# Column-halved first weights and keys, DMA-transposed first keys of the second layer, and a new instruction order

## The chip, the cores and the metric

The kernel runs on one core of one Trainium2 chip. The metric is the device time of one execution in microseconds (us); less is better. A core has five instruction queues that run side by side: PE (TensorE, matmuls; its weight loads are shown as PEld), DVE (VectorE), ACT (ScalarE), POOL (GpSimd) and SP (SyncE, which only issues DMAs). Each queue runs its own list strictly in order, and an instruction whose semaphore is not yet up holds everything behind it on its queue.

## The reference

Input `A_x` is 2048 tokens of 512 features in bf16. Four sublayers follow, each a layer norm, a mixing step and a residual: A, B, A, B. Both passes of A and both of B use the same weights.

```python
# A: 32 heads of 16; the tokens are 4 segments of 512
q, k, v = heads(x @ wq), heads(x @ wk), heads(x @ wv)
for s in range(4):
    p = softmax(qs @ ks.T * 0.25 + causal mask)        # inside the segment
    a_mem = (phi(qs) @ M) / (phi(qs) @ z + 1e-6)       # phi(t) = t+1 or exp(t)
    o = g * a_mem + (1 - g) * (p @ vs)
    M, z = M + phi(ks).T @ vs, z + sum(phi(ks))
x = x + concat(o) @ wo
# B: linear attention over all tokens with feature maps
phi_q, phi_k = [softmax(q w), softmax(-q w)], [softmax(k w), softmax(-k w)]
x = x + ((phi_q @ (phi_k.T @ v)) / (phi_q @ sum(phi_k) + 1e-6)) @ wo
```

## The kernel before, in words

**Tiles.** Tokens lie in 16 tiles of 128, four per segment. `X` holds all of them in SBUF. For a segment, `ln` normalises the four tiles (statistics, `xn`) and turns them feature-major, by PE transposes and a copy out of PSUM where `by_pe` says so, otherwise by a DMA transpose from the SP queue. `a_proj` makes keys, queries and values of a segment; `a_att` does scores, exponentials and the products with the values; `a_out` the output projection and the residual. `b_keys`, `b_queries` and `b_out` do the same for B; B's output needs the sums over all tokens, so `b_out` of a layer can start only when `b_keys` has seen the last segment. "Layer" below means one A and one B.

**Keys.** Scores run on 32-row strips of the array, so the keys of even and odd heads are kept apart, zeros in between: `K[:, par, g, token]`, par 0 or 1, g one of four feature groups of 128. There are two ways to fill it. The direct way (`by_pe=(0, 1)`, the first two tiles of the first segment of both layers): PE computes keys feature-major (`kfm`, 16 matmuls of 128 columns a tile) and three scaled copies out of PSUM (`kfm.copy`, L905 and L906) mask them into K; because the values phi(k) need token-major keys too, PE computes the keys a second time (`k`), with `phi_sum` behind it. The other way, all other tiles: PE computes keys token-major (`k`), a copy spreads them into `ktok` (`k.copy`, L563), and a DMA transpose issued by SP writes K (`kT`). A copy `kp` of the diagonal part goes to `KP` in both. In the direct way queries are computed a tile at a time (`q`, 16 matmuls of 128 columns), in the other a pair of tiles and half of the groups at a time (8 matmuls of 256 columns, twice).

**Scores.** A unit of `stages` is 1024 columns of scores for two pairs of PSUM banks; ACT takes two exponentials of 128 x 1024 for it (L1102, 288 in all). In a first segment unit 0 holds the scores of query tile 1 against the odd keys of tile 0 for all four groups; units 1 to 4 hold the diagonals of one group each and the rest.

**Order.** No scheduler runs on the chip. `ORDER` lists all operations by number, in the order in which they join their queues; `ENGINE` gives a letter for each operation that may run on one of several engines (copies out of PSUM on ACT or DVE, masks on DVE or POOL, stores on ACT or SP); `SLOTS` gives buffers. Negative numbers in `ORDER` are dummy matmuls on a tile `warm` of zeros (L1430, `-408` is 25 of them); they wait for the memset of `warm` (operation 20, DVE, L686), and they stand first in the PE queue, ahead of the first transposes. Operations 81 and 82 are the two DVE memsets that clear `ktok` (L751).

**Start.** `setup` loads the first four tiles of x, then the weights of A from the ACT and SP queues: `wk` as two halves of its rows, then `wq` and `wv` in the same way.

Of the kernel before, what the change touches and what calls it, by code (L numbers as in the profile page):

```python
# [14 lines left out]
D = 512  # L15
# [18 lines left out]
    0, 21, 24, 25, 20, 35, 26, 34, 27, 22, 28, 29, 33, 1, 81, 23, 10, 82, 12, 4, 5, 2, 3, 6, 7, 37, 53, 13, 54, 55, 60, 61, 62, 11, 56, 63, 57, 9,  # L34
    -408, 58, 74, 64, 30, 40, 31, 32, 8, -72, 65, 36, 38, 59, 75, 413, 84, 85, 66, 76, 45, 77, 103, 18, 104, 86, 87, 67, 115, 116, 83, 96, 97, 68,
    69, 41, 414, 78, 42, 105, 117, 46, 88, 17, 106, 39, 70, 47, 98, 159, 79, 160, 71, 48, 107, 72, 80, 89, 49, 161, 73, 323, 50, 134, 91, 133, 110,
    121, 90, 325, 324, 92, 135, 93, 136, 326, 327, 328, 177, 142, 178, 179, 94, 140, 139, 143, 102, 95, 137, 145, 144, 146, 147, 162, 122, 182, 141,
    108, 123, 180, 329, 109, 330, 51, 19, 124, 163, 167, 207, 165, 111, 118, 183, 212, 208, 164, 166, 332, 99, 334, 52, 333, 112, 100, 125, 119, 168,
    184, 101, 127, 44, 120, 181, -40, 192, 197, 335, 193, 130, 185, 186, 131, 171, 172, 187, 113, 336, 128, 169, 138, 114, 170, 416, 126, 417, 331,
    1112, 188, 132, 214, 189, 229, 173, 194, 148, 209, 337, 174, 129, 230, 231, 199, 14, 210, 362, 198, 195, 213, 190, 363, 191, 364, 149, 232, 726,  # L40
    150, 196, 211, 175, 15, 201, 200, 368, 216, 1105, 176, 215, 202, 43, 338, 369, 339, 203, 366, 424, 341, 204, 353, 233, 237, 365, 217, 218, 219,
    253, 220, 151, 205, 370, 258, 152, 153, 374, 375, 221, 206, 154, 234, 254, 372, 371, 238, 727, 415, 376, 244, 245, 426, 246, 367, 373, 427, 342,
    343, 428, 418, 344, 235, 354, 429, 355, 340, 236, 347, 222, 241, 242, 419, 356, 359, 155, 243, 420, 239, 156, 226, 247, 248, 240, 421, 262, 260,
    264, 259, 16, 724, 227, 735, 377, 249, 733, 228, 250, 265, 256, 425, 263, 266, 725, 251, 255, 252, 728, 729, 436, 257, 223, 224, 225, 261, 437,
    434, 345, 389, 435, 438, 439, 267, 360, 386, 274, 268, 346, 279, 269, 348, 270, 731, 349, 440, 441, 271, 357, 442, 286, 361, 275, 276, 287, 387,
    277, 288, 430, 378, 281, 388, 431, 379, 380, -70, 283, 383, 422, 390, 391, 272, 285, 734, 1113, 278, 273, 736, 423, 730, 392, 350, 737, 295, 284,
    351, 395, 280, 358, 732, 289, 290, 396, 452, 453, 157, 296, 397, 384, 282, 1114, 158, 398, 300, 399, 307, 455, 297, 454, 298, 308, 385, 291, 738,
    739, 404, 405, 456, 292, 400, 463, 309, 304, 401, 305, 1103, 402, 406, 464, 410, 352, 411, 293, 457, 299, 310, 458, 302, 311, 306, 301, 303, 574,
    742, 412, 740, 312, 466, 465, 381, 313, 408, 382, 579, 432, 460, 461, 467, 294, 393, 314, 315, 1104, 575, 1106, 433, 407, 548, 403, 459, 549,
    559, 564, 552, 580, 743, 462, 316, 553, 577, 581, 409, 394, 560, 582, 744, 741, 468, 550, 556, 562, 558, 745, 557, 537, 551, 538, -35, 604, 576,  # L50
    469, 578, 320, 539, 321, 748, 566, 317, 318, 322, 605, 609, 631, 561, 749, 319, 583, 445, 584, 585, 563, 586, 565, 587, 471, 472, 610, 443, 588,
    567, 446, 636, 444, 447, 632, 750, 589, 594, 568, 569, 448, 570, 571, 751, 752, 799, 1107, 590, 606, 591, 643, 753, 644, 645, 607, 800, 763, 608,
    611, 612, 754, 595, 450, 449, 473, 801, 546, 572, 592, 764, 593, 613, 614, 547, 615, 616, 765, 628, 802, 638, 573, 617, 542, 778, 544, 618, 543,
    540, 451, 555, 629, 596, 787, 598, 767, 788, 597, 630, 545, 599, 640, 766, 641, 633, 541, 634, 642, 635, 600, 601, 755, 474, 475, 476, 602, 603,
    477, 746, 1115, 768, 1108, 790, 620, 811, 619, 664, 665, 1109, 1110, 812, 478, 621, 666, 756, 637, 813, 757, 485, 789, 486, 761, 646, 747, 647,
    760, 488, 652, 779, 762, 639, 479, 653, 657, 780, 554, 781, 775, 648, 649, 487, 655, 480, 661, 784, 662, 654, 650, 758, 470, 651, 658, 776, 663,
    656, 622, 623, 659, 777, 660, 682, 625, 624, 803, 814, 626, 683, 627, 816, 817, 667, 668, 489, 684, 1116, 782, 481, 815, 673, 678, 674, 669, 670,
    482, 685, 680, 671, 490, 483, 672, 818, 675, 493, 494, 686, 676, 706, 677, 687, 679, -40, 688, 681, 707, 491, 484, 495, 785, 786, 819, 689, 708,
    694, 804, 695, 699, 690, 691, 1111, 820, 697, 821, 769, 1117, 692, 693, 696, 698, 492, 703, 704, 701, 770, 805, 771, 700, 702, 1130, 806, 807,
    705, 935, 709, 1119, 822, 1118, 710, 711, 712, 496, 500, 773, 501, 497, 936, 937, 809, 759, 953, 713, 714, 772, 808, 498, 791, 958, 716, 715,  # L60
    774, 1121, 792, 502, 499, 954, 810, 916, 504, 968, 793, 960, 783, 959, 796, 961, 973, 505, 917, 1120, 832, 969, 833, 835, 834, 918, 506, 717,
    797, 1122, 1123, 955, 975, 938, 974, 971, 956, 970, 718, 719, 957, 1124, 939, 943, 972, 721, 503, 720, 823, 983, 722, 962, 723, 825, 976, 984,
    843, 977, 988, 844, 794, 963, 824, 795, 1151, 826, 964, 1142, 965, 836, 941, 798, 940, 827, 828, 966, 942, 945, 1010, 845, 846, 944, 1143, 1015,
    1011, 978, 946, 979, 1157, 980, 967, 1144, 1158, 1007, 947, 981, 830, 1016, 985, 986, 829, 1159, 1131, 948, 1132, 949, 950, 1008, 990, 837, 840,
    1136, 1009, 831, 982, 1125, 951, 1133, 952, 838, 1022, 1137, 927, 928, 929, 989, 987, 1012, 1145, 1023, 1138, 841, 1017, 992, 993, 991, 1024,
    930, 1019, 925, 1139, 842, 1020, 1013, 919, 1021, 994, 995, 865, 866, 926, 920, 996, 847, 854, 1014, 997, 921, 1018, 1031, 923, 867, 868, 855,
    507, 922, 924, 998, 1140, 1036, 1025, 1026, 839, 1043, 1032, 1027, 1028, 1146, 1141, 1172, 999, 1147, 1044, 1045, 1173, -36, 1040, 873, 1000,
    1029, 848, 1174, 851, 852, 1030, 874, 869, 857, 1034, 1033, 1042, 1041, 1037, 1038, 870, 1035, 1175, 849, 1166, 856, 871, 1061, 1063, 1039, 853,
    1062, 858, 1167, 1046, 850, 1047, 1134, 1160, 875, 1048, 1135, 1168, 1052, 1049, 872, 1057, 1050, 1051, 1001, 1002, 1064, 1053, 1003, 1004, 859,
    1066, 1058, 1005, 1169, 1065, 1055, 1161, 1006, 1162, 1181, 1054, 1056, 1073, 1163, 1059, 1074, 1183, 1148, 1149, 1182, 1067, 1078, 860, 1060,  # L70
# [1404 lines left out]
```

## Time and profile before

| | |
|---|---|
| time, median of 3 runs | 445.2 us (444.83 to 445.81) |
| profiled execution, its own time | 445.13 us |
| span of the profiled execution, first to last instruction | 443.4 us |
| granted TensorE clock in it | 1.000 |
| first exponential of layer 1 / of layer 2 starts | 11.93 us / 217.45 us |
| exponentials, ACT L1102 | 288, 283.3 us busy |
| last exponentials of layer 2 end | 385.6 us |

The 1.7 us between span and time lie around the span. In the tables of stages a column gives the busy time of an engine in that stretch and, in brackets, the number of its instructions. In a timeline row stand start, length, engine, line, operation, output and inputs; "x4" means that four neighbours were merged. A duration there holds the engine's own latency, so neighbours overlap; the rows of the chain (start, time, what) hold only what each step added.

### The profile page before, as it was taken

Reading aid. Unit: us, or ns where it says so; the run is one execution under the profiler, and the core shown is the slowest. Engines: PE = TensorE matmul, PEld = TensorE weight load, DVE = VectorE, ACT = ScalarE, POOL = GpSimd, SP = SyncE. Lnnn points to the kernel's source line nnn. Section 1 sums busy time; section 2 is a strip of 40 time slices with the busy share of each in tenths; the row PEclk is TensorE's granted clock in tenths of the full one; section 3 lists DMA queues with packets and bytes.
Section 4 is the critical chain, followed back from the end, with each engine's and each line's share of the span. In section 5 each row is a group of like instructions: output and inputs, shape, how many; then the busy total and the mean of one; then the engine's idle time right before and its main releaser. Section 6 shows DMA issues by size and latency. Waiting matters only on the chain.

```text
span 443.4 us, 18535 instructions
## 1 busy us (share of the span) xinstructions
PE 425.8 (96%) x7942; PEld 296.9 (67%) x8008; DVE 415.2 (94%) x1033; ACT 409.9 (92%) x633; POOL 263.8 (59%) x439
## 2 busy tenths in 40 slices
PE   8999989999999999999999999999999999999996
PEld 7777666666767565757777766766676765675763
DVE  7999999999998989799999999999999989969996
ACT  4999999999999999996899999999999999999730
POOL 5568778767796788320265678575775657834100
PEclk9999999999999999999999999999999999999999
DMA  8999622523245311243344567333422322232396
GB/s 247 244 192 158 96 51 50 98 45 56 49 51 63 60 27 27 50 61 60 73 83 65 75 84 87 74 73 74 50 44 57 68 33 50 27 51 50 72 155 201
DMA packets 115089, 35.82 MB, mean 81 GB/s; under 512 B 106816, under 2 KB 115008, under 8 KB 115008
## 3 DMA queue, kind: packets, MB, share of 16 engines
q1 hardware_dynamic: 112176, 32.14, 43.1%
q10 hardware_dynamic: 2832, 2.50, 1.7%
q8 instruction: 63, 1.03, 1.0%
q14 instruction: 18, 0.15, 0.1%
HBM read 6.32 MB, written 2.10 MB: 19 GB/s over the span
## 4 chain that ended last, share of the span: by engine, by line
ACT 67%; PE 24%; DVE 6%; issue 1%; DMA 1%; ACTq 0%; POOL 0%; DVEq 0%
ACT PT L1102 49%; PE PS L504 22%; ACT Ek L1198 5%; ACT phi L957 2%; ACT phi L932 2%; ACT K L1281 2%; ACT QT L563 1%; DMA WA_k<-in_A_wk_dram 1%; ACT VT L563 1%; ACT K L905 1%; ACT EQ L1281 1%; DVE Vt L1226 1%; PE PS L585 1%; ACT ktok L563 1%; DVE Zk L1209 1%
## 5 line engine op out<-in xcount | busy, mean ns | idle before, releaser
L1102 ACT ACTIVATE PT<-PS 128x1024 bf16<-128x1024 f32 x288 | 283.3, 1113 | 0.5 <-PE PS L504 0.2
L1108 POOL TENSOR_TENSOR D<-PT,modd 128x256 bf16<-128x256 bf16 x128 | 84.8, 673 | 40.9 <-ACT PT L1102 9.2
L1111 POOL TENSOR_SCALAR_AFFINE_SELECT PT<-PT 128x512 bf16<-128x512 bf16 x128 | 80.7, 642 | 35.7 <-DVE D L1108 21.7
L504 PEld LDWEIGHTS PS<-VT,PT 128*128 128x128 bf16 x2048 | 75.0, 96 | 15.8 <-issue 1.7
L504 PE MATMUL PS<-VT,PT 128*128 128x17 bf16 x2048 | 80.2, 171 | 0.6 <-POOL PT L1111 0.3
L504 PE MATMUL PS<-VT,D 128*128 128x17 bf16 x512 | 59.9, 170 | 0.3 <-issue 0.3
L504 PE MATMUL PS<-QT,K 32*128 32x64 bf16 (+2 forms) x2176 | 55.8, 213 | 1.8 <-ACT PT L1102 0.6
L1163 DVE TENSOR_TENSOR X<-X,PS 128x512 bf16<-128x512 bf16 x64 | 42.8, 680 | 2.1 <-PE PS L504 1.3
L785 DVE BATCH_NORM_STATS2 stats<-X 128x6 f32<-128x512 bf16 x64 | 42.7, 681 | 1.0 <-DMA X<-in_A_x_dram 0.7
L504 PEld LDWEIGHTS PS<-VT,D 128*128 128x128 bf16 x512 | 43.2, 96 | 0.0
L504 PEld LDWEIGHTS PS<-QT,K 32*128 32x128 bf16 x2176 | 29.2, 93 | 19.2 <-ACT PT L1102 13.8
L1226 DVE TENSOR_TENSOR Vt<-PS,Zk 128x1024 bf16<-128x1024 f32 (+1 forms) x34 | 38.7, 1154 | 1.1 <-PE PS L504 0.9
L1198 ACT ACTIVATE Ek<-PS 128x512 bf16<-128x512 f32 x64 | 38.1, 674 | 0.7 <-PE PS L504 0.7
L1108 DVE TENSOR_TENSOR D<-PT,modd 128x256 bf16<-128x256 bf16 x128 | 36.3, 310 | 1.1 <-ACT PT L1102 1.0
L504 PE MATMUL PS<-WA_v,xA 128*128 128x256 bf16 x256 | 36.3, 273 | 0.2
L1301 POOL COPY O<-rho 128x512 bf16<-128x512 bf16 x28 | 16.5, 618 | 32.9 <-DMA OT<-O 12.0
L1205 POOL TENSOR_TENSOR Vt<-Ek 128x512 f32<-128x512 bf16 x24 | 27.7, 1157 | 12.4 <-ACT Ek L1198 9.1
L504 PE MATMUL PS<-WA_k,xA 128*128 128x256 bf16 x256 | 34.9, 273 | 0.1
L504 PE MATMUL PS<-xA,WA_q 128*128 128x256 bf16 (+1 forms) x288 | 34.6, 261 | 0.1
L504 PE MATMUL PS<-WA_o,OT 128*128 128x512 bf16 x110 | 29.4, 380 | 2.1 <-issue 0.6
L1137 DVE TENSOR_TENSOR O<-PS,r 128x256 bf16<-128x256 f32 (+1 forms) x72 | 27.7, 389 | 1.1
L504 PEld LDWEIGHTS PS<-WA_v,xA 128*128 128x128 bf16 x256 | 22.6, 97 | 7.5 <-issue 1.3
(163 smaller groups left out, 925.0 us busy)
## 6 DMA issues: line engine op xcount, KB each, us to landing
X<-in_A_x_dram SPq DMA_DIRECT2D x3, 512.0 KB, 8.9
out_dram<-X ACTq DMA_DIRECT2D x11, 128.0 KB, 2.2
EQ<-in_B_wqkv_dram SPq DMA_DIRECT2D x2, 512.0 KB, 6.0
out_dram<-X SPq DMA_DIRECT2D x5, 128.0 KB, 2.2
OT<-O SPq DMA_TRANSPOSE x36, 3.2
WB_o<-in_B_wo_dram SPq DMA_DIRECT2D x1, 512.0 KB, 6.0
WA_o<-in_A_wo_dram SPq DMA_DIRECT2D x1, 512.0 KB, 4.9
WB_v<-in_B_wqkv_dram SPq DMA_DIRECT2D x1, 512.0 KB, 4.9
```

Of the source, the lines that this page charges most:

```text
L504: return e.matmul(o, l, r, start=st, stop=sp, tile_position=(basep(l), basep(o)))
L563: emit = {"act": lambda e: e.activation(dst(), src(), ACT.Copy), "dve": lambda e: e.tensor_copy(dst(), src())}
L785: self.dve(lambda e, t=t, src=src: e.bn_stats(self.stats[:, t, :], src()), 0.603, [held() if held else R("X", t)], [R("stats", t)], name=" ...
L1102: self.act(lambda e, st=st, pt=pt: e.activation(pt.ap[:].rearrange("p b c -> p (b c)"), self.ps[:, st.slot[0] * 512:st.slot[0] * 512 + 102 ...
L1108: self.either(lambda e, d=d, k=k, pt=pt: e.tensor_tensor(d.ap[:, :, k, :].rearrange("p b (z c) -> p b z c", z=2), self.ends(pt.ap[:, :, 25 ...
L1111: self.pool(lambda e, q=quarters: e.affine_select(q(), q(), [[0, 4], [1, 128]], ALU.is_ge, 0.0, base=0, channel_multiplier=-1), 0.6, [pt() ...
L1137: self.dve(lambda e, r1=r1, view=view, nt=nt, g=g, o=o[ts]: e.tensor_tensor(o.ap[:, 0:nt, g, :].rearrange("p i (h d) -> p i h d", d=DH), v ...
L1163: self.dve(lambda e: e.tensor_tensor(X[:, t, :], X[:, t, :], self.bank(gen), ALU.add), 0.6, [R("X", t), gen()], [R("X", t)], name="resid")
L1198: self.act(lambda e, sgn=sgn, Ek=Ek, gen=gen: e.activation(Ek.ap[:, sgn, :], self.bank(gen), ACT.Exp, scale=1.0 - 2.0 * sgn), 512, [gen()] ...
L1205: self.pool(lambda e, Ek=Ek, sums=sums: e.tensor_tensor(sums(), *(Ek.ap[:].rearrange("p s (h j) -> p s h j", h=H)[:, :, :, 8 * k:8 * k + 8 ...
L1226: self.dve(lambda e, w=w, n=n, Vt=Vt, Zk=Zk, gen2=gen2: e.tensor_tensor(self.signed(Vt)[:, w, :, 0:16], self.bank(gen2).rearrange("p (h d) ...
L1301: P.add(("act", "pool"), {"act": lambda e, dst=dst, src=src: e.activation(dst(), src(), ACT.Copy), "pool": lambda e, dst=dst, src=src: e.t ...
```

## The change: what it does

1. `setup`: `wk` and `wq` come by halves of their columns (feature groups 0-1, then 2-3; rows of 512 bytes in place of 1024). ACT issues x, the second half of `wk`, beta, the first half of `wk`, x; SP issues x, `w_phi`, x and both halves of `wq`.
2. First segment of layer 1, tiles 0 and 1: the direct keys are made by halves of the groups, each with its own PSUM tile and three copies of half the size; queries come from the 256-column form, and a query half waits for its half of `wq` only. Six more operations.
3. First segment of layer 1, scores: unit 0 now holds groups 0 and 1, both parities, of query tile 1; units 1 to 4 take the rest.
4. First segment of layer 2, tiles 0 and 1: `by_pe` is dropped, so the keys go by `ktok` and a DMA transpose like all others. The four `kfm` groups of PE, six `kfm.copy` and two `q.copy` of the direct form go; two `k.copy`, two DMA transposes on SP and two `q.copy` of the paired form come; `phi_sum` (four operations) becomes `phik` (three). Eight operations fewer.
5. `ORDER`, `ENGINE` and `SLOTS` are new throughout. What they say, counted:

| | before | after |
|---|---|---|
| instructions on PE groups / ACT / DVE / POOL / SP | 1171 / 649 / 1033 / 435 / 119 | 1165 / 640 / 1043 / 428 / 127 |
| ACT without DMAs: before first exp; first to last exp of layer 1; between; first to last exp of layer 2; after | 10; 222; 73; 247; 80 | 11; 225; 80; 230; 83 |
| masks of odd heads on DVE / POOL | 128 / 128 | 137 / 119 |
| stores on ACT / SP | 11 / 5 | 5 / 11 |
| first operations of the DVE queue | 20 (`warm`), 35, 34, 33, 81, 82 (`ktok`), statistics | 81, 82 (`ktok`), 20 (`warm`), 33, statistics |

Between the first and the last exponential of layer 1, ACT gets five 512-column copies that DVE had and one small one (`bk.z`), and gives three copies to DVE. Between those of layer 2 it loses four `v.copy`, one `k.copy`, one `q.copy`, one `kp`, two exponentials of keys (`phi.exp`), two `xnT.copy`, three `lo`, two pairs `lnv`/`rs`, a `bk.z` and a `bq.ln`, and gets one `v.copy` and two `lo`; of these the two `phi.exp` (now `phik.exp`), two `xnT.copy`, two pairs `lnv`/`rs`, a `v.copy` and a `lo` now stand ahead of the first exponential of layer 2, a `bq.ln` stands behind the last, and the others went to DVE or POOL. On PE, ahead of the first scores of layer 2, stand three more groups `bo` (8 matmuls of 136 columns), four more of `bout` (2 of 512), two of `v` and four of `k` (4 of 256 each) and two tile transposes; the 32 `kfm` matmuls go, and one `bq` (2 of 512) moved into layer 1.

```diff
 ORDER = (
-    0, 21, 24, 25, 20, 35, 26, 34, 27, 22, 28, 29, 33, 1, 81, 23, 10, 82, 12, 4, 5, 2, 3, 6, 7, 37, 53, 13, 54, 55, 60, 61, 62, 11, 56, 63, 57, 9,
+    26, 27, 0, 21, 81, 82, 28, 24, 25, 1, 20, 33, 53, 54, 12, 4, 10, 34, 7, 2, 29, 55, 22, 30, 60, 61, 62, 5, 6, 3, 8, 56, 63, 37, 57, 74, 64, 40,
...
-            for k in "qv" if t else "k":
-                for h, eng in two:
-                    load(eng, self.WA[k][:, 2 * h:2 * h + 2, :], wview(inp["A_w" + k])[:, 2 * h:2 * h + 2, :], [R("WA", k, h)], 0.75 if t else 1.6)
+            for k, h, eng in (("v", 0, "act"), ("v", 1, "sp")) if t else (("k", 0, "act"), ("q", 0, "sp"), ("k", 1, "act"), ("q", 1, "sp")):
+                a, b = (slice(2 * h, 2 * h + 2), slice(0, D)) if t else (slice(0, 4), slice(256 * h, 256 * h + 256))
+                load(eng, self.WA[k][:, a, b], wview(inp["A_w" + k])[:, a, b], [R("WA", k, h)], 0.75)
...
+        first = s == 0 and pris[0] < 0
...
-                gen = self.gen()
-                self.steps(self.fm_mms(W["k"], xnT, tt, gen), self.wa("k") + [xnT(tt)], gen, pre=[K], n=8, name="kfm")
...
+                for hs in ((0,), (1,)) if first else ((0, 1),):
+                    n, w = len(hs), slice(2 * hs[0], 2 * hs[-1] + 2)
+                    gen = self.gen()
...
+                    self.steps(mms, [R("WA", "k", h) for h in hs] + [xnT(tt)], gen, pre=[K], n=8, name="kfm")
...
-            if direct:
+            if direct and not first:
...
-                    self.steps(mms, self.wa("q") + [xnT(tt - 1), xnT(tt)], gen, pre=[qt] + ([t3] if s >= 1 else []), n=4, name="q")
+                    self.steps(mms, [R("WA", "q", h), xnT(tt - 1), xnT(tt)], gen, pre=[qt] + ([t3] if s >= 1 else []), n=4, name="q")
...
+        if s == 0 and self.L == 0:
+            out = [[S(g, par, 0, 1) for g in (0, 1) for par in range(2)]] + [[D(g, 0), D(g, 1), x] for g, x in zip(G, (S(2, 1, 0, 1), S(3, 1, 0, 1), S(2, 0, 0, 1), S(3, 0, 0, 1)))]
...
-                segs = {0: self.a_proj(0, xs[0], [nb - 11.2 + 0.5 * i for i in range(4)], by_pe=(0, 1))}
+                segs = {0: self.a_proj(0, xs[0], [nb - 11.2 + 0.5 * i for i in range(4)])}
```

The other edits rename tags and split the K parts on which a score waits by halves of groups.

More of the change, by code (lines that the diff above doesn't have):

```diff
@@ L776, in ln @@
         R = self.R
+        which = "lnB%d" % c if pool else "lnA%d" % (4 if self.L == 0 and c == 0 and pris[0] > 0 else c)
         pool = pool or self.p_xA
@@ L780, in ln @@
             self.P.pri = pri
-            self.P.tag = (self.L, "ln%d" % c)
+            self.P.tag = (self.L, which)
             for t in (4 * c + i for i in grp):
@@ L1094, in a_att @@
                     i = item[2]
[L1095 removed]
+                    reads += [K(("k", par, z, i, g // 2)) for par in range(2) for z in range(par + 1)] + [K(("both", i)), seg["KP"][i](), seg["q"][i][g // 2]]
                     put(lambda a, g=g, i=i: both(a, g, i), item, i * 128, off, 64)
```

63 lines of the change are left out of this document (33 added, 30 removed), and 302 rows, old and new, of tables (AFTER, ORDER).

## The prediction

> **What bounds the kernel now.** I read the page's busy shares and its chain first, then the stages.
>
> ```profile
> PE 425.8 (96%) x7942; PEld 296.9 (67%) x8008; DVE 415.2 (94%) x1033; ACT 409.9 (92%) x633; POOL 263.8 (59%) x439
> ACT 67%; PE 24%; DVE 6%; issue 1%; DMA 1%; ACTq 0%; POOL 0%; DVEq 0%
> ...
> 12.00:26.00 14.00, 13.37 (x271) 10.79 (x269) 13.82 (x46) 13.98 (x20) 8.86 (x16) 1.00 1.18 242
> 26.00:185.00 159.00, 152.41 (x3236) 105.99 (x3261) 149.96 (x383) 158.60 (x210) 118.30 (x187) 1.00 0.42 68
> 205.00:221.00 16.00, 15.73 (x254) 12.39 (x255) 15.81 (x36) 12.46 (x30) 3.15 (x6) 1.00 0.30 59
> 221.00:250.00 29.00, 28.39 (x517) 21.71 (x520) 28.35 (x81) 28.94 (x43) 17.01 (x28) 1.00 0.58 89
> 250.00:385.00 135.00, 131.29 (x2698) 90.86 (x2720) 128.87 (x328) 134.93 (x180) 92.07 (x150) 1.00 0.38 58
> ```
>
> The columns after the stretch are PE, PEld, DVE, ACT and POOL. Averaged, PE looks like the bound; by stage it is not. From 12 to 185 and from 221 to 385 us ACT is never idle (158.60 of 159, 134.93 of 135), and the chain is 67% ACT. Between the layers, 205 to 221, ACT is idle 3.5 us while PE and DVE are full: there the order of PE's work decides when the first exponential of layer 2 runs. Hence the rule of this working: in the exponential stages a copy moved onto or off ACT moves the end by its length; between them PE groups count.
>
> **Step 1, the start: +0.5 us.**
>
> ```profile
> 2.27 5.31 DMA WA_k<-in_A_wk_dram
> 7.67 1.07 PE PS L504 x16
> ...
> 0.88 0.11 DVE L686 MEMSET warm<- 128x64 uint32 x1 [0.88 <-PEq L1460]
> 1.04 5.18 PE L1430 MATMUL PS<-warm 128*128 128x240 bf16 x25 [1.04 <-DVE warm L686]
> 1.80 0.48 DVE L751 MEMSET ktok<- 128x512 uint32 x1
> 5.65 0.40 DVE L801 TENSOR_SCALAR xn<-X,mv,rstd 128x512 bf16<-128x512 bf16 x1
> 6.11 0.61 PE L585 MATMUL PS<-ident,xn 128*128 128x128 bf16 x4
> 6.51 0.77 PE L1430 MATMUL PS<-warm 128*128 128x240 bf16 x4
> 6.76 0.60 ACT L563 ACTIVATE xA<-PS 128x512 bf16<-128x512 bf16 x1 [1.39 <-PE PS L585]
> ```
>
> The halves are no shorter a road. PE still makes all four key groups and all queries of both tiles ahead of the first score, in the same PE time, and ACT still has both query copies ahead of the first exponential. What could come earlier is the start of the keys, now at 7.67; but the weights (2.27 + 5.31 = 7.58) only just miss the copy of x (6.76 + 0.60 = 7.36), so at most 0.3 us are there. Column halves are twice as many pieces, half as long, for the same bytes; no row prices that, and 0.5 us of the delay below would cover it.
>
> Against that stands the order of DVE. Both `ktok` memsets now precede `warm`: 2 x 0.48, and up to 0.2 of handing over, so the 25 dummies start some 1.1 us later, and PE must pass them before its first transpose. They take 5.18 for 25, 0.2 each, so they would end near 7.3, where `xn` (5.65 + 0.40) waits since 6.05. The four after them already end quicker. If PE quickens at the same moment as now, near 6.9, the dummies end near 7.05 and the first transpose is 0.9 late; the copy of x then ends near 8.1 to 8.2, 0.5 after 7.67. If it quickens only later, they end at 7.3, and the first transpose (0.4, from 6.11 to 6.51), four more dummies (0.8) and the second transpose (0.4) follow at the slow pace: keys at 8.9, 1.2 late. Bounds: -0.3 to +1.2; I take +0.5, since at present the pace changes while dummies run. On DVE the small copy `lo` of the first tile now waits for the copy of x, with statistics and key copies behind it; PE needs those pieces only for the first score, 3.6 us after the keys start (32 and 32 matmuls, 0.056 each by the row of step 3), which I count as cover.
>
> [...]
>
> **Step 2, layer 1's exponentials: +1.2 us.** The chain gives the ACT price of each kind:
>
> ```profile
> 218.68 0.20 ACT rstd L792
> 218.88 0.52 ACT KP L923
> 220.31 0.58 ACT xA L563
> 220.89 0.18 ACT rstd L791
> 223.11 0.49 ACT phi L813
> 223.60 0.30 ACT xA L892
> 224.82 0.52 ACT VT L563
> 229.52 0.49 ACT QT L563
> ...
> 195.02 0.46 ACT L1218 ACTIVATE Vt<-Zk 128x64 bf16<-128x64 f32 x1
> ```
>
> Five copies come and three go: 2 x 0.52 = 1.04, and a `bk.z` of at most 0.46. DVE, which these relieve, was full only from 12 to 26. Bounds: 0 (ACT's copies let DVE give back waits that hide in the ACT rows) to 1.5.
>
> **Step 3, between the layers: +4.1 us to the first exponential.**
>
> ```profile
> 209.36 0.64 PE L504 MATMUL PS<-Rkv,K 128*128 128x136 bf16 x8
> 209.84 0.39 PE L585 MATMUL PS<-ident,O 128*128 128x128 bf16 x4
> 210.06 0.64 PE L504 MATMUL PS<-Rkv,K 128*128 128x136 bf16 x8
> 210.53 1.89 PE L504 MATMUL PS<-WB_o,OT 128*128 128x512 bf16 x8
> 212.26 0.39 PE L585 MATMUL PS<-ident,xn 128*128 128x128 bf16 x4
> 213.18 1.50 PE L504 MATMUL PS<-xA,WA_k 128*128 128x128 bf16 x24
> 214.52 1.06 PE L504 MATMUL PS<-xA,WA_q 128*128 128x128 bf16 x16
> 216.85 0.40 PE L504 MATMUL PS<-QT,K 32*128 32x128 bf16 x16
> 217.45 1.02 ACT L1102 ACTIVATE PT<-PS 128x1024 bf16<-128x1024 f32 x1
> 224.03 0.60 PE L504 MATMUL PS<-WA_k,xA 128*128 128x256 bf16 x4
> 224.47 0.60 PE L504 MATMUL PS<-WA_v,xA 128*128 128x256 bf16 x4
> ...
> L569 SPq DMA_TRANSPOSE K<-ktok x28: 1231/1324/2455, 14.9 to 352.5; - x28
> ...
> DMA to landing us min/median/max: 3.0/3.7/6.2
> ```
>
> From start to start, a `bo` takes 0.48 (209.36 to 209.84), a transposed tile 0.22 (209.84 to 210.06), a 512-column matmul 0.216 (210.53 to 212.26 for 8), a group of four 256-column matmuls 0.44 (224.03 to 224.47), a `kfm` matmul 0.056 (213.18 to 214.52 for 24). New ahead of the first score: 3 x 0.48 + 8 x 0.216 + 6 x 0.44 + 2 x 0.22 = 6.25; gone: 32 x 0.056 + 2 x 0.216 = 2.2. Net +4.1, so the first score moves from 216.85 to 220.9 on this profile's clock. Bounds: +3.2 (0.3 us that PE shows idle, and about 0.6 of waits shorter than its latency, get filled) to +5.
>
> The DMA keys hide behind that. The first tile's keys leave PE near 212.26 + 0.22 + 6 x 0.216 + 0.22 + 0.88 = 214.9; a copy of 0.49 and 3.7 to landing make 219.2, before 220.9. The second tile is a `bo` and two groups, 1.36, later: 220.6, then a `KP` copy (0.52 on ACT, on POOL somewhat more), against a second score at 222.9 (0.25 for the first, 8 x 0.216 of `bout`). The cover is 1.7 us each; with the longest landing, 6.2, it is gone and costs 0.8. SP issues two more transposes of 1.3 ahead of `b_out`'s, on a queue that waits for its producers anyway: free unless its next transpose is already due.
>
> **Step 4, layer 2's exponentials: -6.3 us.** What the table of the change lists as gone from ACT: four `v.copy` 2.08, `k.copy`, `q.copy` and two `phi.exp` 1.96, `kp` 0.52, two `xnT.copy` 1.07, three `lo` 0.90, two pairs `lnv`/`rs` 0.76, and 0.2 to 0.7 for `bk.z` and `bq.ln`: 7.5 to 8.0. What comes: 0.52 + 0.60. Net -6.3 to -6.9; I take -6.3. DVE must bear it: it takes up three `v.copy`, a `k.copy`, a `q.copy` and four masks, and loses kp's, half-copies of keys and `phi_sum`, about even. It shows 0.65 us idle to 250 and 6.1 to 385, for a stage that is to be 2.2 shorter. Bounds: -4.1 (DVE does not let the stage shrink) to -6.9.
>
> **Step 5, the tail: 0.** PE carries it from 385.6 on with the same groups; a dummy fewer is 0.1.
>
> ```profile
> 385.62 1.37 PE PS L504 x20
> ...
> by line: PE PS L504 80.1%; ACT PT L1102 8.7%; PE PS L585 3.0%; PE PS L1430 1.5%; DVE X L1163 1.1%; issue 0.9%; ACT EQ L1281 0.8%
> ```
>
> Stores moved to SP free ACT's queue where ACT is idle; if they held `b_out`'s last transposes, each would cost SP an issue, near 0.5. Bounds -0.5 to +0.7.
>
> **Sum.** 0.5 + 1.2 + 4.1 - 6.3 = -0.5 against 445.13 of the profiled execution, 0.07 below the median: 444.6, call it 444.5. All bounds at once give -5.0 to +4.8; they will not fall together.
>
> **The rivals.**
> A, the road is shorter than its parts: ACT's copies in layer 1 pay for themselves in DVE's waits (12 to 26 both engines are full), step 2 is 0, and the weights come early enough that the start costs nothing. 445.1 + 4.1 - 6.3 = 442.9. For it: the chain passes through DVE between 14 and 26. Against it: ACT shows no idle time there to recover.
> B, slower: DVE paces layer 2. Its queue gets copies that were ACT's; if its idle 6.8 us are waits inside an ordered list that cannot close, step 4 gives only what the late first exponential takes, -4.1, and the sum is +1.7: 446.8. It decides once more than 1.4 of the 2.2 us by which the stage is to shrink stay in it: the sum is then above +0.9.
> C, the halves do what they say: keys start on half of `wk` before 7.4, and the first exponential comes 0.6 earlier (two of four key groups, 16 x 0.056 less 0.3 of the copy of x) rather than 0.5 later: 443.5. Against it, PE's order above.
> D, PE stays slow through its first transposes, as worked out in step 1: +1.2 in place of +0.5, the sum +0.2: 445.3, no change. For it: 25 dummies at one slow pace, five microseconds of them. Against it: the four that follow are already quicker. [...]
>
> **How the numbers follow.** A change of 0.2%, 0.9 us, is about what can be told from none. The forecast (443.6 to 445.6) has 0.42, A 0.17, C 0.10, B 0.22, D 0.09. Faster than 444.3: A, C and four tenths of the forecast, 0.44; within: the rest of the forecast, D and a little of B, 0.36; slower 0.20. Eight in ten lie between 442.5 and 446.8.
>
> **What would show it.** Start: dummies begin near 2.2 and keys near 8.2. Layer 1: last exponential 1.7 later. Layer 2: first exponential near 223.3 on its own clock, first two K transposes landed before their scores, the exponential stage about 6 us shorter, DVE fuller than 96% there. The forecast is wrong if ACT shows waits for DVE or K after 221, or if the dummies end before 6.3.

## The result, and the profile after

The changed kernel takes 448.67 us (median; 447.28 to 449.81) where the kernel before takes 445.2: a ratio of 1.0074 with a 95% interval from 1.0058 to 1.009. That is 3.3 us slower by the ratio, 3.5 by the medians. Timed a second time (e14 below) it was 448.61 against 444.95, ratio 1.0079 [1.0064, 1.0095]. The prediction was 444.5, with a range from 442.5 to 446.8. It was wrong, and on the wrong side.

The page of the profile after (span 446.8 us, time 448.67): first the busy shares, then the shares of the chain by engine.

```profile
PE 424.9 (95%) x7877; PEld 295.0 (66%) x7940; DVE 416.3 (93%) x1043; ACT 408.8 (91%) x630; POOL 259.0 (58%) x432
...
ACT 57%; PE 24%; DVE 10%; DMA 4%; POOL 2%; issue 2%; ACTq 0%
```

Every engine but DVE has less to do than before (PE 425.8 to 424.9, ACT 409.9 to 408.8), and yet the span is 3.4 us longer: the loss is not work. In the chain, DMA went from 1% to 4% and DVE from 6% to 10%, ACT from 67% down to 57%. So one looks for places where the end now hangs on a transfer. The quickest way is to cut both traces at the same five events. These rows are the exponentials (PT) of ACT in the timeline, start and duration first; before:

```profile
11.93 1.93 ACT L1102 ACTIVATE PT<-PS 128x1024 bf16<-128x1024 f32 x2
...
181.35 2.00 ACT L1102 ACTIVATE PT<-PS 128x1024 bf16<-128x1024 f32 x2
...
396.80 2.02 ACT L1102 ACTIVATE PT<-PS 128x1024 bf16<-128x1024 f32 x2
```

and after:

```profile
14.25 1.94 ACT L1114 ACTIVATE PT<-PS 128x1024 bf16<-128x1024 f32 x2 [0.24 <-PE PS L507]
...
183.58 3.88 ACT L1114 ACTIVATE PT<-PS 128x1024 bf16<-128x1024 f32 x4
...
226.18 4.68 ACT L1114 ACTIVATE PT<-PS 128x1024 bf16<-128x1024 f32 x5
...
399.83 1.99 ACT L1114 ACTIVATE PT<-PS 128x1024 bf16<-128x1024 f32 x2
```

The first exponential of layer 1, the end of its last (181.35 + 2.00; 183.58 + 3.88), the first of layer 2 (217.45, quoted in the prediction; 226.18) and the end of its last give five stages. (The table ahead of the prediction puts the end of the last exponentials at 385.6; the row above puts it at 398.8. At 385.6 the chain passes from ACT to PE, while ACT has ten more exponentials to do.) The same cut through the traces of the runs below that bear on the account (us; "clock" is the mean granted TensorE clock):

```
                                        start  layer 1  between  layer 2  tail   span   clock
before                                  11.93  171.42   34.10    181.37   44.56  443.38  1.0
before, second look (e12)               11.90  171.23   34.09    181.37   44.55  443.14  0.999
before with the change's start (e9)     12.95  171.24   34.10    181.37   44.57  444.22  1.0
after                                   14.25  173.20   38.73    175.65   45.00  446.83  0.996
after, second look (e14)                13.92  172.18   38.53    176.00   45.38  446.01  1.0
after, start as before (e1)             13.08  172.20   38.84    175.86   44.99  444.96  1.0
after, halves at their best (e13)       13.47  172.17   38.53    176.02   45.21  445.39  0.999
after, needed half first (e4)           13.24  172.16   38.84    175.65   45.88  445.76  1.0
```

Before to after: +2.3, +1.8, +4.6, -5.7, +0.4, together +3.4. The two looks at the kernel before agree in every stage within 0.2, so these differences are no scatter of the old kernel. The two looks at the changed kernel differ by 1.0 in layer 1, where the first had a lower clock, and by up to 0.4 elsewhere. Cut where the prediction cuts layer 2, at the 278th exponential (385.57 before, 388.74 after), its stage gives -5.6 and the rest +0.3, so the account is the same. The shape is what was forecast, a late layer 2 that is then made up; but the start, forecast at +0.5, is +2.3, and in this profile every other term is a little worse than its price.

The start, in the chain of the profile after (start, duration, what), and the wait in the PE timeline:

```profile
1.24 0.46 ACTq L574
...
2.34 7.20 DMA WA_k<-in_A_wk_dram
9.54 0.14 issue
9.67 1.96 PE PS L507 x32
```

```profile
2.24 5.18 PE L1442 MATMUL PS<-warm 128*128 128x240 bf16 x25 [2.24 <-DVE even L709]
...
7.80 0.60 ACT L566 ACTIVATE xA<-PS 128x512 bf16<-128x512 bf16 x1 [0.41 <-PE PS L588]
...
9.67 1.95 PE L507 MATMUL PS<-xA,WA_k 128*128 128x128 bf16 x32 [1.27 <-DMA WA_k<-in_A_wk_dram]
...
13.79 0.40 PE L507 MATMUL PS<-QT,K 32*128 32x128 bf16 x16 [0.20 <-DVE K L915]
```

The dummies begin at 2.24 and x is copied at 8.40, both near the forecast. But then PE stands for 1.27 us, waiting for `wk`. Both column halves go out on ACT's queue, at 1.24 and at 2.34. By the landing events of the trace the one issued at 1.24 was in at 6.73; the other took 7.20 us. And the first key group of PE's order reads the other: the new `ORDER` issues op 4 (the later half of the groups) ahead of op 2 (the half PE makes first). Cutting the weights in halves to start on the first one cannot help when the first one comes last. The first score, in the last row, then waits 0.20 us more, for key copies on DVE.

Between the layers and in the tail, PE now waits for two DMA transposes that land late. Chain rows of both and the PE row behind the first:

```profile
211.68 5.22 DMA OT<-O
...
423.64 5.05 DMA PT<-PT
428.69 0.14 issue
428.83 2.32 PE PS L507 x10
```

```profile
216.95 1.47 PE L507 MATMUL PS<-WB_o,OT 128*128 128x512 bf16 x6 [0.39 <-DMA OT<-O]
...
225.72 0.40 PE L507 MATMUL PS<-QT,K 32*128 32x128 bf16 x16
```

Layer 2's exponential stage, by stretches (columns as in the prediction):

```profile
221.00:250.00 29.00, 28.55 (x536) 21.76 (x541) 28.44 (x77) 28.28 (x42) 15.41 (x27) 1.00 0.60 99
250.00:385.00 135.00, 130.56 (x2677) 89.69 (x2701) 129.44 (x334) 134.33 (x179) 93.31 (x149) 1.00 0.36 60
```

ACT is nearly as full as before (134.93 to 134.33 of 135) and DVE hardly fuller (128.87 to 129.44): DVE bore the copies. From 221 to 402 us ACT waits 1.0 us in all, for PE and not for DVE or K.

### The profile page after: what moved, and what is told of

The parts are those of the page before. It is cut to its first block, busy times and chain, and to the rows that moved or that the text cites. A ratio compares the mean times of both kernels' runs of the same rounds, so it can differ in the third digit from the quotient of the medians.

```text
span 446.8 us, 18418 instructions
## 1 busy us (share of the span) xinstructions
PE 424.9 (95%) x7877; PEld 295.0 (66%) x7940; DVE 416.3 (93%) x1043; ACT 408.8 (91%) x630; POOL 259.0 (58%) x432
## 4 chain that ended last, share of the span: by engine, by line
ACT 57%; PE 24%; DVE 10%; DMA 4%; POOL 2%; issue 2%; ACTq 0%
ACT PT L1114 43%; PE PS L507 23%; ACT Ek L1210 5%; ACT phi L967 2%; ACT K L1293 2%; ACT EQ L1293 2%; DMA WA_k<-in_A_wk_dram 2%; DVE Vt L1238 1%; DMA OT<-O 1%; DMA PT<-PT 1%; ACT phi L942 1%; ACT VT L566 1%; DVE xn L805 1%; DVE X L1175 1%; POOL D L1120 1%
## 5 line engine op out<-in xcount | busy, mean ns | idle before, releaser
L1120 POOL TENSOR_TENSOR D<-PT,modd 128x256 bf16<-128x256 bf16 x119 | 78.4, 669 | 36.3 <-ACT PT L1114 13.7
L507 PEld LDWEIGHTS PS<-VT,PT 128*128 128x128 bf16 x2048 | 73.5, 96 | 16.3 <-ACT PT L1114 1.8
L1120 DVE TENSOR_TENSOR D<-PT,modd 128x256 bf16<-128x256 bf16 x137 | 37.8, 300 | 0.5 <-ACT PT L1114 0.3
L507 PE MATMUL PS<-xA,WA_q 128*128 128x256 bf16 x256 | 35.0, 280 | 0.1
L507 PE MATMUL PS<-WA_v,xA 128*128 128x256 bf16 x256 | 34.6, 273 | 0.0
L801 POOL TENSOR_TENSOR rstd<-rstd,negh 128x2 f32<-128x2 f32 (+1 forms) x30 | 22.6, 756 | 9.5 <-DVE rstd L799 8.1
```

The source lines that it names most:

```text
L507: return e.matmul(o, l, r, start=st, stop=sp, tile_position=(basep(l), basep(o)))
L801: self.pool(lambda e, ve=ve, n=n: e.tensor_tensor(ve, ve, self.negh[:, 0:1].to_broadcast([128, n]), ALU.pow), 0.36 + 0.15 * n, res + [R("n ...
L1120: self.either(lambda e, d=d, k=k, pt=pt: e.tensor_tensor(d.ap[:, :, k, :].rearrange("p b (z c) -> p b z c", z=2), self.ends(pt.ap[:, :, 25 ...
```

## Experiments

All are variants of the two kernels; `ORDER` lists operations by number in the order in which each engine's queue is filled. The time of the kernel before, on the same chip as each run, is 445.08 (e1 to e4), 445.28 (e5 to e8), 445.2 (e9 to e12) and 444.95 (e13, e14).

**e1, the start put back.** Op 20 is the dummies' memset, 81 and 82 the two `ktok` memsets.

```diff
-            for k, h, eng in (... ("k", 0, "act"), ("q", 0, "sp"), ("k", 1, "act"), ("q", 1, "sp")):
-                a, b = (slice(2 * h, 2 * h + 2), slice(0, D)) if t else (slice(0, 4), slice(256 * h, 256 * h + 256))
+            for k, h, eng in (... ("k", 0, "act"), ("q", 0, "act"), ("k", 1, "sp"), ("q", 1, "sp")):
+                a, b = slice(2 * h, 2 * h + 2), slice(0, D)
 ORDER: loads 0,1,12,4,10,7,2,5,6,3 -> 0,1,12,10,6,7,2,4,3,5; op 20 ahead of 81, 82
```

> The changed kernel with its start put back: weights by halves of rows, one half on ACT's queue and one on SP's behind the second pair of x tiles, and the memset of the dummies first on DVE. Keys and queries still in half copies, all else of the change kept. Theory 1 (the start costs 2.3 us, and all of it reaches the end): keys begin near 7.7, first exponential near 12.0 to 12.3, time about 448.67 - 2.1 = 446.5. Rival (the start is absorbed: what is saved there comes back as waits in the ordered lists of layer 1, and the loss lies in the later stages): first exponential near 12.2 but last exponential of layer 1 within 0.7 of 187.45, time 448.0 to 448.7.

Measured 446.75 us (12 runs; ratio to before 1.0037 [1.0023, 1.0051]): 1.9 less than the changed kernel, and still 1.7 slower than before. In its chain the weights were still last, a late draw:

```profile
2.27 6.14 DMA WA_k<-in_A_wk_dram
8.41 0.09 issue
8.50 1.96 PE PS L506 x32
...
13.08 1.94 ACT PT L1113 x2
```

Theory 1 holds for the time. Its 13.08 was above the 12.0 to 12.3 expected; in five more profiles with this start (e5 to e8, e11) the first exponential came at 12.62, 12.11, 12.46, 12.13 and 12.47.

**e2, columns on two queues.** e1 with the column slices kept.

> As the run before, but the weights by halves of columns (512-byte pieces). It differs from that run in nothing but the pieces and in that a key group waits for its own half. Theory 1 (the smaller pieces move fewer bytes per us, 0.19 to 0.28 MB in place of 0.35 while they run): halves of wk land near 8.3 to 8.8, keys begin 0.6 to 1.1 later than in the run before, time 447.1 to 447.5. Rival (the pieces don't matter; what was late in the changed kernel was the queue and the order of issue): halves land within 0.3 of the run before, the first group begins as soon as x is copied, first exponential not later than there.

447.13 us (1.0037 [1.0025, 1.0048]). The halves of `wk` landed at 8.73 and 8.93, keys began at 9.06 and the first exponential came at 13.92. The later landing is 0.5 behind e1's, and 1.35 behind the median of nine profiles with row halves (given with e14). So the landings are those of theory 1: on two queues the column halves were late too. In time e1 and e2 cannot be told apart (446.75, 447.13), so the price of the pieces themselves, apart from their order, stays open between 0 and 1.

**e3, dummies first only.**

```diff
 ORDER: 26, 27, 0, 21, 81, 82, ... 1, 20, ... -> 26, 27, 0, 21, 20, 81, 82, ... 1, ...
```

> The changed kernel, with the memset of the dummies ahead of the two ktok memsets on DVE and nothing else. The dummies begin near 1.05 and the first tile of x is copied near 7.4. Theory 1 (the weights are the later of the two, 9.54 against 8.40 for the copy of x): keys still begin near 9.6, first exponential within 0.3 of 14.25, time within 0.5 of 448.67. Rival (the dummies cost the start, as the prediction priced it): first exponential 1.0 earlier, time 447.6.

449.37 us, no gain. PE waited 1.15 us for `wk`, which landed at 8.71 here, so the first exponential was 0.8 earlier than in the first profile of the changed kernel, though the weights still set it. All four executions had a granted clock of 0.992 to 0.996, which costs about a microsecond by itself (last section); against the executions of the changed kernel with such a clock, 449.1 on average, the 449.4 of these four is no gain. Neither theory had these numbers.

**e4, the needed half first.**

```diff
 ORDER: ... 12, 4, 10, 34, 7, 2, ... -> ... 12, 2, 10, 34, 7, 4, ...
```

> The changed kernel with the two column halves of wk swapped on ACT's queue, so that the half of the groups that PE makes first is issued first (at 1.24, where the other half landed at 6.73), and nothing else. Theory 1 (PE waits 1.27 us for a half that was issued last): the first key group begins near 8.45, at the copy of x, the second half lands near 9.5 and holds the second group; the four groups end near 10.9 in place of 11.6, first exponential 0.5 to 0.8 earlier, time 0.5 to 0.8 less. Rival (the order of the halves is no matter, PE needs both at once): first exponential within 0.2 of 14.25 and the time unchanged.

447.45 us, 1.2 less than the changed kernel, by a swap of two numbers. Part of that is the clock, which was full in all four executions; against the executions of the changed kernel at full clock, 447.9 on average, it is 0.5 less, the lower end of theory 1. The needed half landed at 4.86; PE made all four groups from 7.96 on in 2.07 us, nearly without a stop. But the first exponential came only at 13.24: behind the keys the chain ran through another transfer, as e13 shows.

**e5, the first score earlier.** Base: e1.

```diff
 ORDER: 2317, 2318, 2319 (bo) moved behind 1746 (exp); 2314, 2315, 2316 (bo) behind 1752 (exp); 1706, 1705 (lo, v.copy) behind 1746
```

> The first experiment's kernel (the change with its start put back, 446.75 us) with two of layer 1's output groups (bo, PE 0.48 us each, and their divisions and norms on DVE) moved behind layer 2's first exponentials, and one lo copy and one v.copy of ACT (0.42 and 0.51) behind the first of them. Theory (PE's and ACT's order between the layers sets layer 2's first exponential, and what is won there reaches the end because ACT has no idle time after it): first exponential 0.8 to 1.2 earlier against the last exponential of layer 1 (38.8 us after it now), time 445.6 to 446.1. Rival (the exponentials behind it are held by something else, the moved groups or their banks): first exponential earlier, but the exponential stage that much longer, time within 0.3 of 446.75.

452.86 us, 6.1 slower than e1; part of that is the clock, which was below 0.997 in four of the five executions. The first exponential did come 1.0 earlier against layer 1's last (37.86 in place of 38.84), and the stage behind it grew from 175.86 to 181.44. The row of ACT's waits from 228 to 402 us:

```profile
ACT PT L1113 <- PE PS L506: 5.0, 4, 2.9
```

So the exponentials waited for scores. That the moved groups held PSUM banks which those scores needed is likely, and not shown. A microsecond won at the head of an ordered list was paid for five times behind it.

**e6 and e7, three copies to ACT, three to DVE.** Base: e1; single letters in `ENGINE`.

```diff
 e6: v.copy 1687, 1963, 2023: d -> a
 e7: v.copy 1987, 2393, 2429: a -> d
```

> The first experiment's kernel with three v.copy of layer 2 back from DVE on ACT (0.52 us each), where the kernel before had them. Theory (ACT has no idle time there, so a copy counts its length): layer 2's exponential stage 1.4 to 1.6 longer, time 448.1 to 448.4. Rival (DVE paces that stage as well, so that ACT's copies give DVE back what they cost): stage longer by less than 0.7, time 446.8 to 447.4.

> The first experiment's kernel with three more v.copy of layer 2 moved from ACT to DVE. Theory (ACT alone paces, DVE has 5 us of idle time in 135): the stage 1.3 to 1.6 shorter, time 445.2 to 445.6. Rival (DVE is full by now, and each further copy delays the D, O and PhiK that PE and ACT wait for): the stage shorter by less than 0.5 or longer, ACT shows waits for DVE or PE, time 446.4 or above.

e6: 451.22 us (the clock was below 0.997 in all five executions), layer 2's stage 179.55, 3.7 longer than e1's for 1.56 us of copies. e7: 447.32 us, stage 177.14, 1.3 longer where it should have been 1.5 shorter. Waits of PE and then of ACT, 228 to 402 us, in e6:

```profile
PE PS L506 <- ACT VT L565: 3.6, 2, 2.8
...
ACT phi L941 <- DVE ktok L565: 1.9, 1, 1.9
```

and of ACT, then PE, in e7:

```profile
ACT PT L1113 <- PE PS L506: 1.4, 4, 0.5
ACT VT L565 <- PE PS L506: 1.3, 1, 1.3
...
PE PS L506 <- DVE VT L565: 0.9, 1, 0.9
```

In the stage both ways lose; in time e7 (ratio 1.0043 [1.0028, 1.0058]) cannot be told from e1. e7's numbers are those of its rival, e6's are those of neither theory. e1 has none of these waits for VT or ktok: a copy that changes its engine without changing its place in the list arrives at another time, and PE or ACT stands for it. The ledger of copies did foretell the whole change's stage to 0.6 and 0.9 us in the two looks, with an order made for it; for three copies moved inside a given order it failed both times.

**e8, one more transpose on SP.** Base: e1; a transpose of a tile of `wo` into a spare tile, behind op 1365.

> The first experiment's kernel with one more DMA transpose (a 128x512 tile of wo into a spare tile that nothing reads) on SP's queue near 160 us. In the changed kernel and in all four runs so far the same transposes by their place in SP's queue take 4.1 to 7.2 us in place of 3.0 to 3.3 (the 59th, 62nd, 70th, 71st, 81st, 82nd, 98th, 99th, 110th and 111th among them); PE waits for the 59th (0.4) and the 110th (0.2 to 1.1). Theory (the delay belongs to a place in the queue, counted in what was issued before): from the 52nd on the slow places fall one transpose of the kernel earlier, so boT of the second group (now 59th) and the first PT of the tail (now 110th) land in 3.0 to 3.4 unless they are second of a slow pair, PE's waits there go, time 0.3 to 0.9 less than 446.75. Rival (the delay belongs to what else the kernel moves at that moment): the same tiles stay slow, time 446.5 to 447.0.

446.37 us, no clear difference from e1, though it is a time that the theory allowed. The landings speak against the theory. The same tiles stayed slow: boT of the second group took 5.02 us, the first PT of the tail 5.41, one place further down the queue. So the place in the queue is not the cause.

**e9, the change's start alone, on the kernel before.**

```diff
+                    a, c = (slice(2 * h, 2 * h + 2), slice(0, D)) if k == "v" else (slice(0, 4), slice(256 * h, 256 * h + 256))
+                    load({"k": "act", "q": "sp"}.get(k, eng), ...)
 ORDER: loads 0,1,10,12,4,5,2,3,6,7 -> 0,1,12,3,10,5,2,7,4,6; ops 81, 82 ahead of 20
```

> The kernel before with the change's start alone: both halves of wk by columns on ACT's queue, the later groups first, both halves of wq by columns on SP's, in the change's order among the x tiles, and the two ktok memsets ahead of the dummies on DVE. Keys, queries, scores and all behind them as before, keys waiting for both halves. Theory (the start alone costs the changed kernel some 2 us, and no later stage gives it back): keys begin near 8.7 to 9.6 in place of 7.67, first exponential 13.0 to 13.9, time 446.3 to 447.2. Rival (the kernel before has slack behind its start, DVE being late there anyway): first exponential later, but the last of layer 1 within 0.4 of 183.35, time 444.8 to 445.6.

446.36 us (10 runs, 1.0031 [1.0012, 1.005]), 1.2 slower than before. The chain:

```profile
0.97 0.49 DVE ktok L751
...
2.24 5.18 PE PS L1430 x25
7.42 0.43 PE PS L584 x4
7.85 0.48 PE PS L1430 x4
8.33 0.22 PE PS L584 x4
8.55 0.13 issue
8.68 1.07 PE PS L503 x16
```

Two delays end together here. Memsets, dummies and transposes follow one another, as step 1 of the prediction had traced it; x is copied at 8.48 and the transposes end at 8.55. The later half of `wk` lands at 8.59. Keys begin at 8.68 in place of 7.67, and e9 cannot say which of the two set them. The first exponential is 1.02 later, and from there to the end every stage equals the old kernel's within 0.2: nothing behind gives the start back.

**e10, weights back, dummies late.** e1 without the move of op 20.

> The first experiment's kernel with the two ktok memsets ahead of the dummies again: loads as before, dummies 1.1 us late. With the third experiment (dummies early, loads of the change) it makes the square of the two. Theory (whichever of weights and copied x is later starts the keys; weights by rows land near 8.2 to 8.4, the late dummies end near 7.4 and x is copied at 8.4): keys begin 8.4 to 8.6, no later than in the first experiment by more than 0.3, time within 0.4 of 446.75. Rival (the prediction's price of the dummies, 0.5 to 1.2, holds beside the weights): keys near 9.0, time 447.3 to 447.9.

446.96 us: e1's time within its scatter. `wk` landed at 7.54, earlier than its theory had it, x was copied at 8.22, keys began at 8.27 and the first exponential came at 12.86. So here the late dummies alone set the keys, 0.6 behind the 7.67 of the kernel before. With e3, whose keys waited for `wk` until 8.85, this closes the square: taking away one delay leaves the other.

**e11, stores as before.** Base: e1; the engine letters of eight stores.

> The first experiment's kernel with the 16 stores divided between ACT's and SP's queues as the kernel before has them (11 and 5, in place of 5 and 11). Theory (the tail's extra 0.4 to 0.9 us are PE's wait for a PT transpose that lands 4.8 to 5.7 us after its issue, well ahead of the first store): tail within 0.3 of the 44.99 of that kernel, time within 0.4 of 446.75. Rival (stores on SP hold the last transposes): tail 0.5 or more shorter, time 446.2 or less.

447.38 us, tail 45.11, as in the profiles with 11 stores on SP (44.77 to 45.88): no sign that the stores lengthen the tail. The time is 0.2 above what the theory allowed; the clock was below 0.998 in all four executions, which would explain it.

**e12, the kernel before, second look.**

> The kernel before once more, unchanged, for a second profile: how far landing times and stage lengths differ between two executions of one program. If the weights' landing at 7.58 is typical, wk lands within 0.3 of it and the first exponential is within 0.3 of 11.93; if it is a lucky one, wk lands at 8.2 to 8.4 as in the first experiment and the first exponential comes near 12.6. Layer 1's stage 171.2 to 171.7 where the granted clock is 1.0.

`wk` landed at 7.53 (7.58 at first), first exponential 11.90. One point of the trace differs: the granted clock was full from 5.02 on, in the first look from 6.89.

**e13, the halves at their best.**

```diff
 ORDER: ops 2 and 4 swapped as in e4; op 20 ahead of 81, 82; key group 103 (second tile, first half) behind 84
```

> The changed kernel with three things put right for its halves: the half of wk that PE makes first is issued first, the dummies come first on DVE, and PE makes the first half of the groups of both tiles before the second half of either. Theory A (the halves never had anything to win here: the copy of x at 7.4 starts the keys, as in the kernel before, and the queries come after all four groups; the later half, landing near 8.5, is just in time): keys begin near 7.4 to 7.9, first exponential 12.2 to 12.7, time 446.0 to 446.8, as good as the first experiment with its halves of rows and no better. Theory B (done in the right order, the halves do what the change says): first exponential before 11.9, that of the kernel before, and time 445.6 or less.

448.17 us (1.0071 [1.0058, 1.0084]), no better than the changed kernel. Keys did begin at 7.85, as early as before, and still the first exponential came at 13.47. The chain:

```profile
2.83 6.96 DMA X<-in_A_x_dram
9.79 0.02 issue
9.81 0.69 DVE stats L788
...
13.02 0.43 PE PS L506 x16
```

With the weights ahead of it in ACT's queue, the third tile of x is issued at 2.83 (1.72 in the kernel before) and lands at 9.79 (5.79 before). DVE's list has that tile's statistics ahead of its share of the key copies, so the score waits for DVE. Neither theory had this; theory B falls, and theory A's time is missed by 1.4. The start of the change holds three delays side by side, of 0.6 (the dummies, e10) to 1.3 us (PE's wait for `wk`): whichever is removed, the next one shows.

**e14, the changed kernel, second look.**

> The changed kernel once more, unchanged, beside the run before it on the same chip. Theory A (the landing of the later half of wk differs from execution to execution; the 9.54 of the first profile was late, the 8.5 to 8.7 of the other kernels with this order is usual): it lands at 8.4 to 9.0, first exponential 13.2 to 13.8, time 447.4 to 448.4. Theory B (9.5 belongs to this kernel): lands at 9.3 to 9.8, first exponential near 14.2, time 448.4 to 449.0.

448.61 us, the later half at 9.22, first exponential 13.92: nearer to theory B. Over six profiles with this order of issue (after, e3, e4, e9, e13, e14) the half issued second landed at 8.47 to 9.54, median 8.83; over nine with row halves on two queues at 7.44 to 8.41, median 7.58. The one profile with column halves on two queues (e2, 8.93) lies among the six, so the queue alone does not account for the difference.

## Why the prediction was wrong, step by step

Step 1, the start, is the step that failed: +0.5, bounds -0.3 to +1.2, against +2.3 and +2.0 in the two profiles. It looked at two delays and priced one. The dummies it traced rightly: 2.24 where "near 2.2" was forecast, and where the weights are in early (e10) x is copied at 8.22 and keys begin 0.6 late, with 8.1 to 8.2 and 0.5 forecast. The +1.02 of e9 lies inside the bounds too, but holds both delays. Whether a late start pushes the full clock back, on which rival D turns, the clock records leave half open: with dummies from 2.24 on it came at 5.25 to 7.87 us (five profiles, median 7.45; 7.55 in the profile after), with dummies from 1.04 on at 4.18 to 6.89 (eleven, median 5.43; 6.89 in the profile before), later on the whole, with ranges that overlap. What the step dismissed was the weights: "at most 0.3 us are there", and for the twice as many pieces "0.5 us of the delay below would cover it". That sentence took the landing of 7.58 as given and asked only how much earlier it could be. The diff halves the pieces, moves both halves to one queue, the half needed first to its second place, and a tile of x behind them; none of this was worked out. With the half at 9.54 and x copied at 8.40 the cover was not 0.5 us but minus 1.1 (9.22 and 8.36 in the second look, minus 0.9). How much of this is the pieces and how much the place in the queue stays open: e2's halves, on two queues, landed as late. Rival C fell with the same halves; in e13, with the needed half in at 4.77, keys still began behind the copy of x, at 7.85, so it did not win there either. The remaining 0.3 lies between keys and first exponential (7.67 to 11.93 before, 9.67 to 14.25 after); 0.2 of it is the wait of the first score for DVE.

The third part of step 1, the statistics that DVE would do ahead of the key copies, was seen ("statistics and key copies behind it") and called covered by 3.6 us. That cover is gone too: with the tile of x landing at 9.5 to 10.2, PE's first score waits for DVE, 0.2 us in both looks at the changed kernel and 0.8 in e4 and e13.

Step 2, layer 1: +1.2, measured +0.8 to +0.9 at a granted clock of 1.0 (172.18 against 171.42 and 171.23). That fits ACT's copies counting there; no run moves them alone. The other 1.0 of the +1.8 in the first profile (173.20 against 172.18) goes with the fall of the clock.

Step 3, between the layers: +4.1, bounds +3.2 to +5, measured +4.4 to +4.8. The mechanism fits: PE's order sets it, and in e5, with two groups and two copies taken out, the first exponential comes 1.0 earlier. The DMA keys landed before their scores, as forecast (by the trace at 224.34 for a score at 225.72). The missing 0.3 to 0.7 includes 0.2 to 0.5 of PE's wait for boT, a transpose that took 5.22 us where the median of its kind before was 3.2; the working has no term for it.

Step 4, layer 2: -6.3, measured -5.4 to -5.7, within the bounds of -4.1 and -6.9. DVE did not pace it, so rival B, whose time of 446.8 came nearest, was nearest for a reason that did not happen. But the rule that the step rested on, that a copy moved on or off ACT moves the end by its length, failed for the three copies of e6 and the three of e7.

Step 5, the tail: 0, bounds to +0.7, measured +0.4 and +0.8 (+1.3 in e4). e11 shows no cost of the stores; what came instead is PE's wait for the first PT transpose, 0.3 us in the first profile and 0.8 in the second. The step's picture, PE carrying the end from 385.6 on, holds for the kernel before; after, the chain stays on ACT until 397.2 (391.4 in the second look).

So the working was -0.5 where the first profile says +3.4: 1.8 from the start, 0.6 from layer 1 (1.0 of clock, less 0.4), 0.5, 0.6 and 0.4 from the rest, all of one sign. (The bounds as the steps list them add up to -4.5 and +4.3, not to -5.0 and +4.8.) Of the signs it named, the dummies, the landing of K, ACT's waits and the shorter stage came as forecast; the keys (9.67 for 8.2), the first exponential of layer 2 (226.18 for 223.3) and DVE above 96% (129.44 of 135 is 95.9%) did not. e9 shows that the start alone makes the old kernel 1.2 slower, and e1 that taking it out makes the new one 1.9 faster. The 1.7 that remain in e1 are not taken apart by an experiment. In its profile the five stages give +1.2, +0.8, +4.7, -5.5 and +0.4: layer 1, the transition and the tail together cost more than layer 2 gives, and the start is still late, by 0.2 to 0.7 in the five other profiles like it.

## What to carry to other kernels

When a load is cut in halves so that work can begin on the first, write down for each half its queue, its place there and the group that reads it, and do the same for whatever those loads push back: here PE's wait for the weights hung on two numbers in a list, and the tile pushed back was the next limit. In a kernel whose order is written out, price a whole stage by its ledger, but do not expect the ledger to hold for a few operations moved inside a finished order. A cover is the difference of two times: work out both after the change, not one of them before it.

## What the runs showed of the hardware that was not expected

**Half clock for 3.41 us.** In 6 of the 13 profiles with the changed layer 1, and in none of the three with the old one, the granted clock falls to half once, always 88.75 us after it first became full, for 3.41 us (full from 7.55 and half from 96.29 to 99.71 in the profile after). The stretches after (first row below) and in the second look, columns as before, the clock third from the right:

```profile
95.00:100.00 5.00, 5.00 (x89) 3.16 (x88) 3.42 (x11) 4.42 (x5) 1.58 (x4) 0.66 0.29 56
```

```profile
95.00:100.00 5.00, 4.82 (x122) 3.83 (x123) 4.62 (x16) 5.00 (x7) 1.73 (x3) 1.00 0.29 56
```

PE does 89 matmuls in place of 122, and layer 1 takes 173.2 to 173.9 us in place of 172.2 to 172.5. Of 11 timed executions of the changed kernel 6 had a mean clock of 0.996, and they took 449.1 us on average against 447.9 for the others; of the kernel before, 9 of 66. A less busy PE is not enough for it: in the 3.41 us ahead of the fall PE was busy for 0.75 to 0.81 of its time in the six (0.78 in the profile after), but in the kernel before it was busy for 0.71 from 60.41 to 63.82 us, and the clock stayed at 1.00 there and behind. What decides is not shown.

**Small pieces.** Pieces of 512 bytes took 27 ns in the median and those of 1024 bytes 46 (trace, first 9 us), so the same bytes take a sixth longer; but from 4 to 6 us the rate fell further: to 163 to 219 GB/s in all seven profiles with column halves, on one queue or two, where eight of the nine with row halves moved 271 to 306 (the ninth, e1, 208). Before, then after, GB/s last and the engines' busy share ahead of it:

```profile
4.00:6.00 2.00, 2.00 (x12) 1.36 (x9) 1.86 (x8) 1.04 (x3) 0.76 (x2) 1.00 0.96 300
```

```profile
4.00:6.00 2.00, 2.00 (x12) 1.51 (x10) 1.90 (x8) 1.15 (x1) 0.58 (x2) 1.00 0.76 200
```

The engines were not even busy: 14 of the 16 parts of the half of `wk` issued first were in by 4.73, the last at 6.73; why that part came late is not shown. In the second look (e14) the last part of the same half came at 4.62: it differs from execution to execution.

**Transposes beside instruction loads.** The profile counts 63 transfers of 16 KB of instructions, 1.1 us each. DMA transposes that had such a transfer in flight within 3 us of their issue took over 4 us in 26 of 52 cases before and 22 of 53 after; the others in 5 of 45 and 4 of 47 (from 20 us on). That would explain why e8's tiles stayed slow, if the loads come at the same instructions. It is a coincidence in time that no experiment tested.
